# Delta-rule attention and gated experts on one core: column steps of a triangular inverse with the next row by itself, key norms by VectorE from half the number's bits, two spreading copies apart

## The chip, the cores and the metric

The kernel runs on one core of a Trainium2 chip. Its time is the device time in microseconds (us), median of the runs. Engine names are those of the profile: PE (TensorE's matmuls) and PEld (its weight loads), DVE (VectorE), ACT (ScalarE), POOL (GpSimd), SP (the engine that issues most DMAs). Each engine takes its own instructions in the order in which the program gives them, and waits where an instruction needs another engine's result.

## What is computed

Four batches, eight heads, 768 tokens, head size 48. First a delta-rule attention, in which a 48x48 state per head is read and corrected at every token; its key is divided by its own norm:

```python
k_n = k / (np.linalg.norm(k, axis=-1, keepdims=True) + 1e-06)
for t in range(S):
    y[:, :, t] = np.einsum('bhd,bhde->bhe', q[:, :, t], state)
    v_old = np.einsum('bhde,bhd->bhe', state, kt)
    state = state + bt[:, :, :, None] * np.einsum('bhd,bhe->bhde', kt, vt - v_old)
```

The result, as 3072 rows of 384 numbers, goes through a router that picks one of four groups and then one of four experts in that group. Each row is multiplied by its expert's two matrices (384x1024, ReLU, 1024x384) and by the two softmax weights. All of it is in float32.

## The kernel before

**Tiling.** The sequence is cut into NCH = 24 chunks of C = 32 tokens. A chunk holds all four batches (4 x 32 = 128 partitions) and all eight heads. Within a chunk the token-by-token recurrence becomes a lower triangular system of 32x32 per batch and head. Chunks are taken in NGR = 6 groups of RG = 4: the systems of one group, 4 chunks x 8 heads x 4 batches = 128, lie one on each partition, and VectorE inverts them together.

**`gram(u)`** (L209) multiplies chunk u's keys with keys and queries on PE; ACT copies the key part to `gt` (L228), DVE masks the query part into `gq` (L233). Both read one PSUM tile `g_ps`. It shares one buffer (tag "g") with `t_ps` (L385) and `r_ps` (L456), so the next user waits until L233 or L462 has read it.

**`inverse(g)`** (L237) is a generator: a list of steps in which each `yield` hands control back. It transposes `gt` into `m` (L243), takes the squared key norms from the diagonal, then the square root: `max` with a tiny number on DVE (L248), `Sqrt` on ACT (L250), one Newton step on DVE (L252 to L256). It derives the factors `r0` and `norm` (L258 to L270), scales `m` (L272) and prepares `cs` (L277). Then come 30 column steps, j = 1 to 30: a product of column j (rows j+1 and below) with row j (columns 0 to j-1) into `t` (L284), and its addition to the rows below (L288). Every row below j is changed by every step j. Last it multiplies by `cs` (L290), sets the diagonal (L292), transposes into `mt` (L295), and ACT spreads `mt` with two scaled copies into `mtb` (L300), one after the other. Only when `mtb` is there may the next group pass its TURN (L274).

**The period.** `advance(u)` (L315) is chunk u's own work, a chain through PE and ACT: `a_ps` (L321, L327; it reads `vh`, which `scale(u)` makes on DVE at L308) and `f` (ACT L331); `w_ps` from `mtb` (L343) and `w` (ACT L346); the state's update `s_ps` (L353) and `s_bd` (ACT L359, two instructions), which the next chunk's L327 reads; the output `o_ps` (L364) and `x` (ACT L368). Beside it run `logits(u-1)` (L378: `t_ps` on PE, `xt` on ACT L389, `l_ps`, `lg` on ACT L395) and `gram(u+9)`. f(u) below means chunk u's L331; the time from f(u) to f(u+1) is called a period.

**`route(r)`** (L398) is another generator: for a group of four chunks it chooses group and expert with some 25 small DVE instructions. They include `hots` (L448), `rk` (L462), `place` (L464) and `mine` (L484), with an `Exp` on ACT (L459), counting on PE (L456, L457), and, for each chunk, POOL's `at` (L489) and PE's sorting product from `at` and `mine` (L495).

**What sets the order.** Nothing is scheduled by the compiler here: the order of each engine's instructions is the order of the calls. `inverse` and `route` are put into the gaps by `work(n)` (L517). Each call gives every task n x 180 x its rate as credit (rate 0.9 for `inverse`, 0.25 for most `route`); a step is taken while the credit is above zero, and costs 180 plus the number that its `yield` names (L515). A step that yields ACT_STEP, PE_STEP, SOON, NEXT, SORT or TURN waits until the loop calls `allow` with that word. In a period (L579 to L617) the calls are: start of `advance`, `scale(u+1)`, work(16), `w`, allow(SORT), `gram(u+9)`, allow(ACT_STEP), work(9), the mask `gq`, work(8), `s_ps` to `x`, allow(PE_STEP), allow(ACT_STEP), allow(SOON), work(12). `inverse(g)` starts at the end of the period u with u = 4(g-2)+2. Groups 0 and 1 begin ahead of the loop (L552 to L578), where nothing but `gram` stands beside them.

**After the loop** comes the expert stage (L690 to L784): 16 experts in turn, gathering rows by indirect DMA, two matrix products, scattering the results.

Of the kernel before, what the change touches and what calls it, by code (L numbers as in the profile page):

```python
# [8 lines left out]
F32 = mybir.dt.float32  # L9
I32 = mybir.dt.int32  # L10
AX = mybir.AxisListType
ALU = mybir.AluOpType
ACT = mybir.ActivationFunctionType
PSUM = bass.MemoryType.PSUM

C = 32
# [46 lines left out]
def deltanet_then_moe(  # L63
# [13 lines left out]
    nc = tc.nc  # L77
# [76 lines left out]
    with ExitStack() as first:  # L154
# [54 lines left out]
        def gram(u, home=None):  # L209


            g, uu = divmod(u, RG)
            kqt = kqt_[u % NB]
            if uu == 0:
                gts[g] = wk.tile([128, C, RG, H], F32, tag="gt", name=f"gt{g}", bufs=1)
            g_ps = home
            if home is None:
                g_ps = ps.tile([128, 2, 512], F32, tag="g", name=f"g_ps{u}")
            g_out = g_ps.rearrange("p f (j x) -> p (f j) x", j=NP)[:, :, 0:2 * C].rearrange(
                "p h (a t) -> p h a t", a=2)  # L220
            for j in range(NP):
                for b in range(B):
                    for hh in range(2):
                        rows = slice(hh * 64, hh * 64 + D)
                        nc.tensor.matmul(g_out[quads[b], hh * NP + j], lhsT=kqt[rows, 0, j, quads[b]],  # L225
                                         rhs=kqt[rows, :, j, quads[b]], start=True, stop=True,
                                         skip_group_check=True)
            nc.scalar.activation(  # L228
                gts[g][:, :, uu].rearrange("p t h -> p h t"), g_out[:, :, 0, :],
                ACT.Copy)  # L230
            gq = wk.tile([128, H, C], F32, tag="gq", name=f"gq{u}", bufs=LEAD + 1)
            gqs[u] = gq
            return lambda: nc.vector.tensor_tensor(  # L233
                gq, g_out[:, :, 1, :], cut["upper"][:, None, :].to_broadcast([128, H, C]),
                op=ALU.mult)

        def inverse(g):  # L237

            m = wk.tile([128, C, C], F32, tag="m", name=f"m{g}")
            flat = m.rearrange("p i j -> p (i j)")
            nc.vector.transpose(out=flat, in_=gts.pop(g).rearrange("p t u h -> p (t u h)"))  # L243
            yield C * C
            diag = flat[:, ::C + 1]
            nrm, r0, r1 = [sm.tile([128, C], F32, tag=n, name=f"{n}{g}")
                           for n in ("nrm", "r0", "r1")]
            nc.vector.tensor_tensor(r0, diag, cut["tiny"].to_broadcast([128, C]), op=ALU.max)  # L248
            yield ACT_STEP
            nc.scalar.activation(r0, r0, ACT.Sqrt)  # L250
            yield SOON
            nc.vector.reciprocal(r1, r0)  # L252
            yield
            nc.vector.tensor_tensor(r1, r1, diag, op=ALU.mult)
            yield
            nc.vector.tensor_tensor(r0, r0, r1, op=ALU.add)  # L256
            yield
            nc.vector.scalar_tensor_tensor(nrm, in0=r0, scalar=-0.5,  # L258
                                           in1=cut["eps"].to_broadcast([128, C]), op0=ALU.mult,
                                           op1=ALU.subtract)  # L260
            yield
            nc.vector.reciprocal(r1, nrm)
            yield
            nc.vector.tensor_tensor(r1, r1, r1, op=ALU.mult)
            yield
            nc.vector.scalar_tensor_tensor(r0, in0=r1, scalar=-1.0, in1=bt[:, g], op0=ALU.mult,
                                           op1=ALU.mult)
            yield
            norm[g] = sm.tile([128, C], F32, tag="normt", name=f"normt{g}")
            nc.vector.transpose(out=norm[g], in_=nrm)  # L270
            yield
            nc.vector.tensor_tensor(m, m, r0[:, :, None].to_broadcast([128, C, C]), op=ALU.mult)  # L272
            yield C * C
            while g and g - 1 not in mts:  # L274
                yield TURN
            cs = wk.tile([128, C, C], F32, tag="cs", name=f"cs{g}", bufs=1)
            nc.vector.tensor_tensor(cs, cut["below"].rearrange("p (i j) -> p i j", i=C),  # L277
                                    r0[:, None, :].to_broadcast([128, C, C]), op=ALU.mult)
            yield C * C
            for j in range(1, C - 1):  # L280
                n = C - 1 - j
                t = wk.tile([128, C * C // 4], F32, tag="t", name=f"t{g}_{j}")
                tv = t[:, 0:n * j].rearrange("p (i c) -> p i c", i=n)
                nc.vector.tensor_tensor(tv, m[:, j + 1:, j:j + 1].to_broadcast([128, n, j]),  # L284
                                        m[:, j:j + 1, 0:j].to_broadcast([128, n, j]),
                                        op=ALU.mult)
                yield n * j
                nc.vector.tensor_tensor(m[:, j + 1:, 0:j], m[:, j + 1:, 0:j], tv, op=ALU.add)  # L288
                yield n * j
            nc.vector.tensor_tensor(m, m, cs, op=ALU.mult)  # L290
            yield C * C
            nc.vector.tensor_scalar(diag, r0, -1.0, None, op0=ALU.mult)  # L292
            yield
            mt = wk.tile([128, RG * H, C], F32, tag="cs", name=f"mt{g}", bufs=1)
            nc.vector.transpose(out=mt.rearrange("p r i -> p i r"), in_=flat)  # L295
            mtb = wk.tile([128, RG * H, 2, C], F32, tag="mtb", name=f"mtb{g}")
            yield 2 * C * C
            yield ACT_STEP
            for a in range(2):
                nc.scalar.activation(mtb[:, :, a], mt, ACT.Copy,  # L300
                                     scale=cut["parity"][:, a:a + 1])
            mts[g] = mtb
# [204 lines left out]
        def push(task):  # L507
            said = next(task, "end")
            if said == "end":
                behind.remove(task)  # L510
                held.pop(task, None)
                allow(TURN)
            else:
                held[task] = said if isinstance(said, str) else None
                due[task] -= 180 + (said if isinstance(said, int) else 0)  # L515

        def work(n):  # L517

# [10 lines left out]
        def allow(what):  # L529

            for task in list(behind):
                if held.get(task) is what:
                    push(task)
# [4 lines left out]

        with tc.manual_schedule(engines={mybir.EngineType.PE, mybir.EngineType.DVE,
                                         mybir.EngineType.Activation, mybir.EngineType.Pool}):  # L540
            nc.scalar.activation(rooted, cut["tiny"], ACT.Sqrt)
            homes = [None, s_ps[:, 0:2], s_ps[:, 2:4]]
            masks = []
            for u in range(RG):
# [34 lines left out]
            for u in range(NCH + 1):  # L579
                step = advance(u) if u < NCH else iter([None] * 4)  # L580
                turned = logits(u - 1) if u else iter([None] * 2)
                next(step)
                allow(NEXT)
                r = group_of.get(u - 2)
                if r is not None and group_of.get(u - 1) != r and r < NGR - 2:
                    start(route(r), 0.25)
                next(turned)
                if u + 1 < NCH:
                    scale(u + 1)
                work(16)  # L590
                next(step)
                allow(SORT)
                masks = gram(u + LEAD) if u + LEAD < NCH else lambda: None
                allow(ACT_STEP)
                work(9)
                masks()
                work(8)
                next(step)
                next(turned)
                next(step)  # L600
                allow(PE_STEP)
                allow(ACT_STEP)
                r = group_of.get(u - 1)
                if r is not None and group_of.get(u) != r and r >= NGR - 2:
                    start(route(r), 0.6 if r == NGR - 2 else 1)
                allow(SOON)
                if u % RG == RG - 2 and u // RG + 2 < NGR:
                    start(inverse(u // RG + 2), SHARE)
                work(12)
                if u + NB < NCH:  # L610
                    load_kq(u + NB)
                if u + NV < NCH:
                    load_kv(u + NV)
                if u < NCH:
                    nc.sync.dma_start(out=x_dram[u * 128:(u + 1) * 128], in_=xs[u])
                if pieces and u >= RG:
                    pieces.pop(0)()  # L617
# [265 lines left out]
```

## Time and profile before

| what | us |
|---|---|
| median of 3 runs (582.28, 583.00, 584.39) | 583.0 |
| the profiled execution's own time | 588.25 |
| its span, first to last instruction | 586.5 |
| f(0), the first chunk's L331 | 55.3 |
| f(4), f(8), f(12), f(16), f(20) | 97.2, 130.8, 175.5, 212.6, 246.3 |
| f(23), the last chunk's L331 | 270.0 |
| first expert product (L706) | 294.1 |
| DVE busy in the whole span | 251.1 |
| of it L284 and L288, 180 instructions each | 60.3 and 60.0 |

In a timeline row the columns are start in us, duration in us, engine, line, operation, result <- operands with their sizes, and in brackets the idle time before it with what ended it. A duration runs from an instruction's start to its end. Two instructions of one engine may overlap, so the distance from start to start is read beside the duration. The granted clock (PEclk) is the share of full speed at which PE was allowed to run. The mean of the profiled execution was 0.955, but in a stretch it is 1.0 or about a half.

### The profile page before, as it was taken

The page shows a single profiled execution, that of the slowest core. Times are in us where ns is not written, and L with a number is a line of the kernel's source. Part 1 is how long each engine was busy: PE and PEld are TensorE (multiplying, and loading weights), DVE is VectorE, ACT ScalarE, POOL GpSimd, SP SyncE. Part 2 cuts the span into 40 slices and gives each one's busy share as a digit, 9 for nine tenths or more (in the row PEclk, how much of TensorE's full clock was granted, in tenths as well). Part 3 has the DMA queues.
Part 4 walks back from the last instruction along what each step waited for, and adds up shares of the span by engine and source line. Part 5 has one row for each costly group of instructions (what it writes and reads, how often), then busy time and mean ns, then how long its engine had stood idle before and what let it go on. Part 6 is the DMA issues. An engine that isn't in the chain of part 4 may idle for free.

```text
span 586.5 us, 18265 instructions
## 1 busy us (share of the span) xinstructions
PE 503.2 (86%) x8166; PEld 460.1 (78%) x8166; DVE 251.1 (43%) x751; ACT 171.4 (29%) x335; POOL 105.2 (18%) x110
## 2 busy tenths in 40 slices
PE   3213888988999979999599999999999999999993
PEld 2212667767777767778499999999999999999993
DVE  1788997989769879513441011111111111111110
ACT  2102345573564564543011121111111111111110
POOL 0000000002102121121334113414125222221111
PEclk9999998996979989899589999999999999999998
DMA  7990243432421222210126665666756666776400
GB/s 271 403 381 11 83 130 125 160 130 83 143 106 51 90 69 83 82 61 30 36 72 207 181 222 164 215 190 212 249 175 216 213 221 222 242 236 209 169 20 19
DMA packets 44321, 90.64 MB, mean 155 GB/s; under 512 B 9755, under 2 KB 29650, under 8 KB 44240
## 3 DMA queue, kind: packets, MB, share of 16 engines
q1 hardware_dynamic: 34256, 79.71, 40.0%
q0 software_dynamic: 9984, 9.74, 6.2%
q8 instruction: 65, 1.06, 0.8%
q14 instruction: 16, 0.13, 0.1%
HBM read 79.92 MB, written 9.66 MB: 153 GB/s over the span
## 4 chain that ended last, share of the span: by engine, by line
issue 33%; PE 23%; DVE 15%; POOL 12%; DMA 9%; ACT 6%; POOLq 0%; SPq 0%; ACTq 0%
DMA out_dram<-yo,to_i 8%; POOL xg L685 7%; POOL out_dram L736 5%; DVE t L284 4%; DVE m L288 4%; PE a_ps L321 3%; ACT s_bd L359 3%; PE w_ps L343 3%; PE s_ps L353 3%; PE a_ps L327 3%; PE o_ps L336 2%; PE g_ps L225 2%; PE s_ps L495 2%; PE t_ps L385 1%; DMA kqt<-in_kq_dram 1%
## 5 line engine op out<-in xcount | busy, mean ns | idle before, releaser
L706 PE MATMUL h_ps<-xt,w 128*128 128x224 f32 (+14 forms) x768 | 140.4, 337 | 0.6 <-DVE xt L697 0.6
L720 PE MATMUL y_ps<-hid,w 128*128 128x224 f32 (+14 forms) x768 | 138.8, 334 | 0.0
L706 PEld LDWEIGHTS h_ps<-xt,w 128*128 128x128 f32 x768 | 131.3, 192 | 1.6 <-DVE xt L697 0.9
L720 PEld LDWEIGHTS y_ps<-hid,w 128*128 128x128 f32 x768 | 129.3, 190 | 0.3
L697 DVE COPY xt<-t_ps 128x336 f32<-128x336 f32 (+14 forms) x32 | 15.1, 471 | 141.3 <-PE t_ps L695 141.3
L709 ACT ACTIVATE hid<-h_ps 128x448 f32<-128x448 f32 (+14 forms) x64 | 32.3, 505 | 126.9 <-PE h_ps L706 126.9
L735 DVE TENSOR_SCALAR yo<-o_ps,gate 112x384 f32<-112x384 f32 (+14 forms) x32 | 19.6, 616 | 106.3 <-PE o_ps L732 106.3
L284 DVE TENSOR_TENSOR t<-m 128x30 f32<-128x30 f32 (+9 forms) x180 | 60.3, 335 | 4.0
L288 DVE TENSOR_TENSOR m<-m,t 128x30 f32<-128x30 f32 (+9 forms) x180 | 60.0, 334 | 4.5
L685 POOL DMA_INDIRECT xg<-x_dram,from_i x32 | 39.2, 1225 | 115.8 <-PE t_ps L695 100.4
L736 POOL DMA_INDIRECT out_dram<-yo,to_i x32 | 39.2, 1225 | 101.9 <-DVE yo L735 101.0
L321 PE MATMUL a_ps<-vh,con 128*128 128x384 f32 x48 | 26.5, 639 | 33.3 <-DVE vh L308 21.8
L722 ACT ACTIVATE yt<-y_ps 128x224 f32<-128x224 f32 (+14 forms) x48 | 16.2, 338 | 120.2 <-PE y_ps L720 120.2
L359 ACT ACTIVATE s_bd<-s_ps 48x768 f32<-48x768 f32 x46 | 36.9, 803 | 17.6 <-PE s_ps L353 17.0
L321 PEld LDWEIGHTS a_ps<-vh,con 128*128 128x128 f32 x48 | 8.2, 214 | 36.5 <-DVE vh L308 19.9
L489 POOL TENSOR_SCALAR at<-con,place 128x256 f32<-128x256 f32 x20 | 19.9, 1001 | 89.7 <-DVE t L284 36.7
L450 POOL TENSOR_TENSOR acc<-acc,hots 128x16 f32<-128x16 f32 x20 | 5.7, 287 | 147.8 <-DVE hots L448 146.6
L343 PEld LDWEIGHTS w_ps<-f,mtb 64*64 64x64 f32 x768 | 25.6, 139 | 7.1 <-issue 4.9
L343 PE MATMUL w_ps<-f,mtb 64*64 64x48 f32 x768 | 28.9, 224 | 1.7 <-ACT f L331 1.1
L327 PEld LDWEIGHTS a_ps<-s_bd,kqt 128*32 128x32 f32 x736 | 18.1, 125 | 15.5 <-issue 15.5
L353 PE MATMUL s_ps<-w,kv 32*128 32x96 f32 x736 | 28.4, 293 | 0.5 <-issue 0.3
L353 PEld LDWEIGHTS s_ps<-w,kv 32*128 32x128 f32 x736 | 24.4, 198 | 3.1 <-issue 1.0
(115 smaller groups left out, 526.1 us busy)
## 6 DMA issues: line engine op xcount, KB each, us to landing
w<-in_w_dram SPq DMA_DIRECT2D x28, 1536.0 KB, 7.5
kqt<-in_kq_dram SPq DMA_DIRECT2D x24, 512.0 KB, 4.9
kv<-in_kv_dram SPq DMA_DIRECT2D x24, 448.0 KB, 3.4
x_dram<-x SPq DMA_DIRECT2D x24, 192.0 KB, 2.1
w<-in_w_dram SPq DMA_DIRECT2D x6, 512.0 KB, 9.6
w<-in_w_dram SPq DMA_DIRECT2D x4, 576.0 KB, 10.1
w<-in_w_dram SPq DMA_DIRECT2D x2, 384.0 KB, 9.6
con<-in_const_dram SPq DMA_DIRECT2D x1, 512.0 KB, 8.7
```

The lines of the kernel that those rows point to most:

```text
L284: nc.vector.tensor_tensor(tv, m[:, j + 1:, j:j + 1].to_broadcast([128, n, j]), m[:, j:j + 1, 0:j].to_broadcast([128, n, j]), op=ALU.mult)
L288: nc.vector.tensor_tensor(m[:, j + 1:, 0:j], m[:, j + 1:, 0:j], tv, op=ALU.add)
L321: nc.tensor.matmul(a_ps.rearrange("p h d -> p (h d)"), lhsT=ident, rhs=vh.rearrange("p h d -> p (h d)"), start=True, stop=(u == 0), skip_g ...
L327: nc.tensor.matmul(a_ps[quads[b], 2 * j:2 * j + 2, :], lhsT=kqt[:, 0, j, quads[b]], rhs=s_bd[:, b, j], start=False, stop=True, skip_group_ ...
L343: nc.tensor.matmul(w_ps[b, h], lhsT=mt[b, uu * H + (h % 2) * NP + h // 2], rhs=f[b, h], start=True, stop=True, skip_group_check=True)
L353: nc.tensor.matmul(s_at[:, b, j], lhsT=k[quads[b], j], rhs=w[quads[b], 2 * j:2 * j + 2], start=(u == 0 and j == 0), stop=True, skip_group_ ...
L359: nc.scalar.activation(s_bd[rows, :, :, hh, :], s_at[rows, :, :, hh * D:(hh + 1) * D], ACT.Copy)
L685: nc.gpsimd.indirect_dma_start(out=xg[0:P, t, :], out_offset=None, in_=x_dram[:, :], in_offset=bass.IndirectOffsetOnAxis(ap=rows[0:P, t:t ...
L706: nc.tensor.matmul(h_ps[:, k], lhsT=w1[:, j, (f + k) * 128:(f + k + 1) * 128], rhs=xt[:, j], start=(j == 0), stop=(j == DC - 1), skip_grou ...
L709: nc.scalar.activation(hid[:, f:f + 2], h_ps, ACT.Relu)
L720: nc.tensor.matmul(y_ps, lhsT=w2[:, f, j * 128:(j + 1) * 128], rhs=hid[:, f], start=(f == 0), stop=(f == FC - 1))
L736: put = nc.gpsimd.indirect_dma_start(out=out[:, :], out_offset=bass.IndirectOffsetOnAxis(ap=to[0:P, i:i + 1], axis=0), in_=yo[:, :], in_of ...
```

## The change

Line numbers move: after the change, L284 and L288 become L316 and L322, with new lines L294 and L299 in between; L295 becomes L329, L300 L334, L308 L342, L484 L518, L495 L529.

```diff
-            nc.vector.tensor_tensor(r0, diag, cut["tiny"].to_broadcast([128, C]), op=ALU.max)
-            yield ACT_STEP
-            nc.scalar.activation(r0, r0, ACT.Sqrt)
-            yield SOON
+            nc.vector.tensor_scalar(r0.bitcast(I32), diag.bitcast(I32), 0.5, float(0x1fbd1df5),
+                                    op0=ALU.mult, op1=ALU.add)
+            yield
+            nc.vector.reciprocal(r1, r0)
+            yield
+            half = 0.5 * (1 - 3.13e-4)
+            nc.vector.scalar_tensor_tensor(r1, in0=r1, scalar=half, in1=diag, op0=ALU.mult,
+                                           op1=ALU.mult)
+            yield
+            nc.vector.scalar_tensor_tensor(r0, in0=r0, scalar=half, in1=r1, op0=ALU.mult,
+                                           op1=ALU.add)
+            yield
             nc.vector.reciprocal(r1, r0)
...
+            def add_column(j, c):
+                rows = m[:, j + 1:, c]
+                nc.vector.scalar_tensor_tensor(rows, in0=m[:, j + 1:, j], scalar=m[:, j, c:c + 1],
+                                               in1=rows, op0=ALU.mult, op1=ALU.add)
+
+            def add_row(j, i):
+                row = m[:, i, 0:j]
+                nc.vector.scalar_tensor_tensor(row, in0=m[:, j, 0:j], scalar=m[:, i, j:j + 1],
+                                               in1=row, op0=ALU.mult, op1=ALU.add)
+
             for j in range(1, C - 1):
-                n = C - 1 - j
-                t = wk.tile([128, C * C // 4], F32, tag="t", name=f"t{g}_{j}")
-                tv = t[:, 0:n * j].rearrange("p (i c) -> p i c", i=n)
-                nc.vector.tensor_tensor(tv, m[:, j + 1:, j:j + 1].to_broadcast([128, n, j]),
-                                        m[:, j:j + 1, 0:j].to_broadcast([128, n, j]),
-                                        op=ALU.mult)
-                yield n * j
-                nc.vector.tensor_tensor(m[:, j + 1:, 0:j], m[:, j + 1:, 0:j], tv, op=ALU.add)
-                yield n * j
+                n = C - 2 - j
+                if j < 3:
+                    for c in range(j):
+                        add_column(j, c)
+                        yield n + 1
+                elif n < 2:
+                    for i in range(j + 1, C):
+                        add_row(j, i)
+                        yield j
+                else:
+                    t = wk.tile([128, C * C // 4], F32, tag="t", name=f"t{g}_{j}")
+                    tv = t[:, 0:n * j].rearrange("p (i c) -> p i c", i=n)
+                    below = m[:, j + 2:, 0:j]
+                    nc.vector.tensor_tensor(tv, m[:, j + 2:, j:j + 1].to_broadcast([128, n, j]),
+                                            m[:, j:j + 1, 0:j].to_broadcast([128, n, j]),
+                                            op=ALU.mult)
+                    yield n * j
+                    add_row(j, j + 1)
+                    yield j
+                    nc.vector.tensor_tensor(below, below, tv, op=ALU.add)
+                    yield n * j
...
-            yield ACT_STEP
             for a in range(2):
+                yield ACT_STEP
                 nc.scalar.activation(mtb[:, :, a], mt, ACT.Copy,
                                      scale=cut["parity"][:, a:a + 1])
...
-                due[task] -= 180 + (said if isinstance(said, int) else 0)
+                due[task] -= 100 + (said if isinstance(said, int) else 0)
...
-            nc.scalar.activation(rooted, cut["tiny"], ACT.Sqrt)
+            nc.scalar.activation(rooted, cut["tiny"], ACT.Exp)
...
+                allow(ACT_STEP)
                 masks = gram(u + LEAD) if u + LEAD < NCH else lambda: None
-                allow(ACT_STEP)
```

In words, per group of four chunks:

- **The norm.** DVE halves the number's bits and adds a constant, which gives a rough square root, and refines it with one more Newton step (reciprocal, product, sum). ACT's `Sqrt` and the `max` are gone.
- **Column steps.** Steps 1 and 2 are one or two instructions, each of which multiplies a column by one number of each partition and adds it. Steps 29 and 30 do the same by rows. Steps 3 to 28 take three instructions: the product for rows j+2 and below, then row j+1 by itself (product and sum in one instruction), then the addition to rows j+2 and below. That is 84 instructions where there were 60.
- **The two copies into `mtb`** each wait for an allow(ACT_STEP) of their own, and the one in the middle of a period stands ahead of `gram` instead of behind it.
- **The credit** that a step of `inverse` or `route` costs is 100 plus its size instead of 180.
- **The first table** that ACT loads is that of `Exp`.

## The prediction

> **What bounds the kernel now.** First the slices of the span (14.7 us each).
>
> ```profile
> PE   3213888988999979999599999999999999999993
> DVE  1788997989769879513441011111111111111110
> PEclk9999998996979989899589999999999999999998
> ```
>
> DVE is full in the first four slices while PE idles, both are near full up to slice 17, and from slice 20 only PE works. There the expert stage runs PE without a gap (233 of 233 us between 300 and 533), and the change doesn't touch it. Of 586.5 us some 290 are open. PE's clock falls in slices 8, 9, 11 and 14, inside the stage that is open.
>
> Next DVE's timeline, read from start to start.
>
> ```profile
> 22.00 0.42 DVE L233 TENSOR_TENSOR gq<-g_ps,con 128x256 f32<-128x256 f32 x1
> 22.33 0.19 DVE L284 TENSOR_TENSOR t<-m 128x30 f32<-128x30 f32 x1
> 22.55 0.21 DVE L288 TENSOR_TENSOR m<-m,t 128x30 f32<-128x30 f32 x1
> ...
> 106.60 0.40 DVE L284 TENSOR_TENSOR t<-m 128x238 f32<-128x238 f32 x1
> 106.91 0.17 DVE L424 TENSOR_TENSOR gh<-lg,gb 128x16 f32<-128x16 f32 x1
> 107.03 0.41 DVE L288 TENSOR_TENSOR m<-m,t 128x238 f32<-128x238 f32 x1
> ```
>
> A duration is about 157 ns plus 1.04 ns per element. An instruction that needs the one just before starts about 30 ns after that one's end: N elements cost 187 + 1.04N ns (L284 to L288: 0.22). One that doesn't starts while its forerunner still runs: 0.33 after L233, whose 256 elements take 267 ns, so 62 + 1.04N. A stranger between two dependent ones (L424) is free: 106.60 to 107.03 is 0.43, no more than without it.
>
> The prelude, ahead of the first chunk, is DVE alone, but for one wait.
>
> ```profile
> 26.42 0.33 DVE L288 TENSOR_TENSOR m<-m,t 128x168 f32<-128x168 f32 x1
> 30.83 0.42 DVE L233 TENSOR_TENSOR gq<-s_ps,con 128x256 f32<-128x256 f32 x1 [4.08 <-ACT gt L228]
> ...
> 52.53 0.53 DVE L308 TENSOR_TENSOR vh<-kv,normt 128x384 f32<-128x384 f32 x1
> ```
>
> That mask waits for the last early `gram`, which stood 3.48 us in the middle for nothing that the profile shows. Then 21.7 us of DVE to the first `vh`.
>
> In the loop an undisturbed period takes 8.0 us with `gram`, 8.4 with L495 too, 7.7 without `gram`. From f(0) to f(23) the 214.7 us hold some 29 more. Two places carry most of it. ACT in chunk 11:
>
> ```profile
> 165.03 0.49 ACT L346 ACTIVATE w<-w_ps 128x384 f32<-128x384 f32 x1 [0.77 <-PE w_ps L343]
> 166.45 0.62 ACT L228 ACTIVATE gt<-g_ps 128x256 f32<-128x256 f32 x1 [0.92 <-PE g_ps L225]
> 166.86 2.15 ACT L300 ACTIVATE mtb<-mt,con 128x1024 f32<-128x1024 f32 x2
> 169.01 1.28 ACT L250 ACT_TABLE_LOAD   x1
> 170.44 1.62 ACT L359 ACTIVATE s_bd<-s_ps 48x768 f32<-48x768 f32 x2
> ```
>
> Both copies, a table and the root stand ahead of `s_bd`. Elsewhere it follows the end of L228 by 0.55, here by 3.37: 2.8 us late. And PE in chunks 8 and 9:
>
> ```profile
> 135.09 1.06 PE L495 MATMUL s_ps<-mine,at 128*128 128x48 f32 x4 [1.45 <-DVE mine L484]
> 136.07 1.19 PE L225 MATMUL g_ps<-kqt 48*32 48x64 f32 x64
> 137.19 2.04 PE L353 MATMUL s_ps<-w,kv 32*128 32x96 f32 x32
> ...
> 148.60 1.15 PE L353 MATMUL s_ps<-w,kv 32*128 32x96 f32 x32
> ```
>
> A wait of 1.45 us for `mine`, then the same products at half the clock (granted 0.60, 0.50, 0.62 in 134 to 146). From L495 to the next f this took 10.05 us against 6.32 one period later: the low clock cost 3.7. A shorter low stretch (94 to 98) cost 1.3: a_ps 1.65 for 0.91, L327 to L336 1.28 for 0.69.
>
> **Column steps.** A pair costs 374 + 2.08N' ns, N' = j(31-j). Summed over 30 steps (sum of N' 4960) that is 21.5 us per group. In the changed program's order each of the three instructions of a step waits for the one two places before it: the addition for the product, the next product for the row, the row for the last addition. So product to addition costs 187 + 1.04N with the row free between them (62 + 62 + at most 29 is under 187), and addition to next product only 62 + 1.04N: 249 + 2.08N with N = j(30-j). For steps 3 to 28 (sum 4381) that is 6.5 + 9.1 = 15.6 us. The seven others: 1.1. Together 16.7, so **4.9 us less** per group.
>
> The row takes its factor from memory per partition. No row shows that form right behind another. The nearest is L489, also a per-partition factor, 0.18 us after `mine` of 96 elements (62 + 100 ns): no extra. I take none; the upper end is a row that waits for its forerunner and holds its successor, priced below.
>
> [...] Where every one of the 84 pays 187 ns, a group costs 84 x 187 + 9.6 = 25.3 us, 3.8 more than before. The rows above show 62 instead of 187 where nothing depends, and I go by the row.
>
> **Norm.** Four dependent instructions of 32 numbers (three at 0.22, the reciprocal at 0.38) replace L248 and the trip to ACT: 1.04 against 0.49 in group 0, 0.82 in group 1, up to 4.3 with other work between, later. +0.5, +0.2, then a small gain. Halving bits as integers is not in the trace; between 0.19 (other 32s) and 0.31 (an integer shift, L670), I take 0.22. ACT loses five table loads (1.28 each) and six roots.
>
> **Route steps and masks** lose their free places, since the rows occupy them: some 25 at 62 to 130 ns, about 2 us per group. By this spacing in the changed order, four periods with a route cost DVE 31.7 us against 32.9. PE needs 32 to 33.6. DVE just comes clear of PE.
>
> **Copies.** The cheaper credit ends each inverse about half a period earlier. In the new order the first copy stands in chunk 4k+2 between `w` and L228, the second at the end of that period, where they were in 4k+3. The first fits the 0.9 us that ACT idles there, with 0.2 to 0.4 left over; the second (1.09) fits the 1.45 between `x` and the next f, with `Exp` beside it. A late `mt` would hold `gram`'s copy, `s_bd` and PE behind the first one.
>
> **The sum.** *Prelude:* the mask after the product of step 10 is reached at 27.7, waits to 30.83 as before, and then 16.35 us of DVE are left (steps 11 to 28: 4.5 + 6.7; last steps 0.5; masks and rest of step 10: 1.3; L290, L292, L295: 3.3). First `vh` at 47.2 instead of 52.5, f(0) at 50.2. *Chunk 1* waits for its `vh`, behind nine column steps of group 1 where there were seven (a step costs less credit): 11.8 us after the first instead of 11.3. f(1) 63.0, f(2) 71.6. *Chunk 2:* `mt` is ready at 76.3, `w` at 74.7; the first copy waits, s_bd is 1.8 late. f(2) to f(6): 4 x 8.0 + 1.8 = 33.8. *Route pairs:* `mine` can't move, since the mask `gq` ahead of it must wait for chunk 6's own L228 (f(6) + 4.7). Then come 8.25 us: mask 0.33, transpose 1.25, norm 3.65, L272 and L277 2.3, route steps 0.7. So L495 starts at f(6) + 13.0, w_ps being done at + 10.4: PE waits 2.6, and f(8) = f(6) + 13.0 + 6.3 = +19.3. The same in chunks 11 and 15. f(6) to f(10): 19.3 + 16.8 = 36.1; to f(14) 36.4; to f(18) 34.8 (no `gram` from 15); to f(23) 38.5. That gives f(23) = 251.2 at full clock.
>
> [...] I go by the rows: 1.4 for chunk 2 and 2.5 (between 1.3 and 3.7) for each of three waits, 8.9. f(23) = 260.1, 9.9 earlier than 270.0. All behind it moves along: span 576.6, time 578.4 for 588.25. The median of before lies 5.25 under its profiled execution, so 583.0 - 9.9 = **573**.
>
> **Rivals.**
> - *Clock stays up* (the rule, 20%): 573 - 8.9 = 564. For it: DVE and ACT no longer disturb PE elsewhere. [...]
> - *A new wait eats the loop's gain* (20%): each L495 wait and chunk 2 draw the long low stretch, 3.7 each: 573 + 3 x 1.2 + 2.3 = 579. The prelude's 5 stay.
> - *Slower: the flush is paid* (10%): the per-partition factor makes the rows hold their neighbours, so the rule's 25.3 us hold. DVE then needs 32.9 + 3.8 + 0.8 = 37.5 per four periods and bounds the loop, with 1.5 for the mask's wait 39, against 38 on average between f(3) and f(19): +4; prelude +3.4, group 1 +4: 594. It decides from the point at which a step's three instructions cost more than the pair did, 374 + 2.08N'.
> - *It doesn't do what it says* (5%): waits one place apart at run time, or new handshakes cancel the 10 us: 583.
>
> Forecast 45%. A run tells about 0.5% (2.9 us) from no change. Faster: 45 + 20 + 15 of the 579 case = 80%. Same: 5 of that case and 4 of the last = 9%. Slower 11%. The range reaches from 562 (the first rival, less 2 for the low stretch at 278 to 299, which can shift either way) to 580, just past the second; left out are mainly the slower cases.
>
> **What would show it.** From one L322 to the next L316 62 + 1.04N ns, about 0.30 at 225 elements, and L299 hidden. First `vh` near 47. No ACT_TABLE_LOAD past the first. L334 (the copies) in chunks 2, 6, 10 once after `w` and once after `x`, and `s_bd` on time but in chunk 2. `mine` as the releaser of a wait of 2 to 3 us on PE in chunks 7, 11, 15, with low clock behind it. Wrong would make me: steps of 0.5 us more, an L342 that PE waits for in the loop, or a first `vh` later than 50.

## The result, and the profile after

| what | before | after |
|---|---|---|
| median of the runs | 582.8 (4 runs, 582.28 to 584.39) | 582.8 (4 runs, 582.09 to 583.69) |
| the profiled execution's own time, span | 588.25, 586.5 | 582.09, 580.3 |
| f(0), f(3), f(7) | 55.3, 84.9, 121.5 | 51.5, 85.8, 118.6 |
| f(11), f(15), f(23) | 162.7, 201.6, 270.0 | 159.2, 197.8, 264.6 |

The ratio is 0.9996, interval 0.9972 to 1.002: no change, where 573 was forecast, with 562 to 580 as the range. The profiled executions alone differ by 6.2 us. That contradiction is the first thing to explain.

The slices of after, in the order of those shown of before:

```profile
PE   3315779979989899997599999999999999999993
DVE  1889989898898896123531111110111111111110
PEclk9999979989979979998599999999999999999998
```

DVE is as full as before (251.8 us busy for 251.1), but done about one slice earlier: counted from 0, its last high digit is the 6 of slice 15, where before has a 5 in slice 16, and the last group's `mt` starts at 225.09 where it started at 237.58. PE's clock did not get better in the loop: it is low in slices 5, 8, 11 and 14, where before has its low digits in 6, 9, 11, 14 and 16. DVE's timeline shows the new column steps:

```profile
64.22 0.38 DVE L316 TENSOR_TENSOR t<-m 128x224 f32<-128x224 f32 x1
64.53 0.23 DVE L299 SCALAR_TENSOR_TENSOR m<-m 128x14 f32<-128x14 f32 x1
64.67 0.38 DVE L322 TENSOR_TENSOR m<-m,t 128x224 f32<-128x224 f32 x1
64.97 0.38 DVE L316 TENSOR_TENSOR t<-m 128x225 f32<-128x225 f32 x1
```

From L322 to the next L316 it takes 0.30, as forecast. The row takes 0.14 until L322 starts, where 0.08 (62 ns and 14 numbers) was reckoned, so L316 to L322 is 0.45 instead of 0.42, and a step of this size 0.75 instead of 0.715. L322 starts 0.14 behind a row that itself takes 0.23, so the 187 ns are not paid on each instruction.

ACT in chunk 2 and PE in chunk 7:

```profile
76.10 0.49 ACT L380 ACTIVATE w<-w_ps 128x384 f32<-128x384 f32 x1 [0.74 <-PE w_ps L377]
79.30 1.15 ACT L334 ACTIVATE mtb<-mt,con 128x1024 f32<-128x1024 f32 x1 [2.71 <-DVE mt L329]
80.36 0.58 ACT L228 ACTIVATE gt<-g_ps 128x256 f32<-128x256 f32 x1
80.74 1.66 ACT L393 ACTIVATE s_bd<-s_ps 48x768 f32<-48x768 f32 x2
```

```profile
123.96 0.62 PE L529 MATMUL s_ps<-mine,at 128*128 128x48 f32 x4 [2.99 <-DVE mine L518]
...
125.50 2.04 PE L387 MATMUL s_ps<-w,kv 32*128 32x96 f32 x32
127.46 1.47 PE L427 MATMUL l_ps<-wr,xt 128*128 128x20 f32 x6
...
135.43 0.86 PE L225 MATMUL g_ps<-kqt 48*32 48x64 f32 x64
136.22 1.15 PE L387 MATMUL s_ps<-w,kv 32*128 32x96 f32 x32
137.29 0.84 PE L427 MATMUL l_ps<-wr,xt 128*128 128x20 f32 x6
```

In the first, the copy stands behind `w`, waits 2.71 us for `mt`, and L228 and `s_bd` stand behind the copy. In the second, PE waits 2.99 us for `mine`, and the same products as ten microseconds later then take nearly twice as long: L387 2.04 for 1.15, L427 1.47 for 0.84. Two more such waits, 1.66 and 2.48 us, stand in chunks 11 and 15. From L529 to the next f these three took 8.8, 8.5 and 8.1 us. Undisturbed it is 6.32 (chunk 8), and 5.61 without `gram`, which chunk 15 has no more (chunk 16). The low clock (granted 0.58 from 123.9 to 132, 1.00 from 132 to 140) thus cost 2.5, 2.2 and 2.5.

What the change removed is gone: no ACT_TABLE_LOAD after the first, `s_bd` on time in chunks 6, 10 and 14.

### The profile page after: what moved, and what is told of

It is laid out like the page before. It is cut to its first block, busy times and chain, and to the rows that moved or that the text cites. A ratio compares the mean times of both kernels' runs of the same rounds, so it can differ in the third digit from the quotient of the medians.

```text
span 580.3 us, 18417 instructions
## 1 busy us (share of the span) xinstructions
PE 502.1 (87%) x8166; PEld 459.6 (79%) x8166; DVE 251.8 (43%) x913; ACT 164.4 (28%) x324; POOL 105.0 (18%) x110
## 4 chain that ended last, share of the span: by engine, by line
issue 32%; PE 21%; DVE 19%; POOL 12%; DMA 9%; ACT 5%; POOLq 0%; SPq 0%; ACTq 0%; DVEq 0%
DMA out_dram<-yo,to_i 8%; POOL xg L719 7%; POOL out_dram L770 5%; DVE m L322 3%; DVE t L316 3%; PE s_ps L387 3%; PE w_ps L377 3%; PE a_ps L355 3%; ACT s_bd L393 3%; PE a_ps L361 2%; DVE m L299 2%; PE s_ps L529 2%; PE o_ps L370 2%; PE l_ps L427 1%; PE t_ps L419 1%
## 5 line engine op out<-in xcount | busy, mean ns | idle before, releaser
L719 POOL DMA_INDIRECT xg<-x_dram,from_i x32 | 39.3, 1227 | 121.5 <-PE t_ps L729 100.1
L316 DVE TENSOR_TENSOR t<-m 128x81 f32<-128x81 f32 (+13 forms) x156 | 51.3, 329 | 0.2
L322 DVE TENSOR_TENSOR m<-m,t 128x81 f32<-128x81 f32 (+13 forms) x156 | 50.6, 324 | 0.0
L355 PE MATMUL a_ps<-vh,con 128*128 128x384 f32 x48 | 26.2, 633 | 26.0 <-DVE vh L342 15.2
L299 DVE SCALAR_TENSOR_TENSOR m<-m 128x29 f32<-128x29 f32 (+27 forms) x174 | 39.2, 228 | 0.4
L355 PEld LDWEIGHTS a_ps<-vh,con 128*128 128x128 f32 x48 | 8.4, 219 | 28.7 <-DVE vh L342 15.4
L377 PEld LDWEIGHTS w_ps<-f,mtb 64*64 64x64 f32 x768 | 25.3, 138 | 7.0 <-issue 4.9
L387 PE MATMUL s_ps<-w,kv 32*128 32x96 f32 x736 | 28.8, 296 | 0.2
L484 POOL TENSOR_TENSOR acc<-acc,hots 128x16 f32<-128x16 f32 x20 | 5.1, 256 | 129.2 <-DVE hots L482 128.0
```

Of the source, the lines that this page charges most:

```text
L299: nc.vector.scalar_tensor_tensor(row, in0=m[:, j, 0:j], scalar=m[:, i, j:j + 1], in1=row, op0=ALU.mult, op1=ALU.add)
L316: nc.vector.tensor_tensor(tv, m[:, j + 2:, j:j + 1].to_broadcast([128, n, j]), m[:, j:j + 1, 0:j].to_broadcast([128, n, j]), op=ALU.mult)
L322: nc.vector.tensor_tensor(below, below, tv, op=ALU.add)
L355: nc.tensor.matmul(a_ps.rearrange("p h d -> p (h d)"), lhsT=ident, rhs=vh.rearrange("p h d -> p (h d)"), start=True, stop=(u == 0), skip_g ...
L377: nc.tensor.matmul(w_ps[b, h], lhsT=mt[b, uu * H + (h % 2) * NP + h // 2], rhs=f[b, h], start=True, stop=True, skip_group_check=True)
L387: nc.tensor.matmul(s_at[:, b, j], lhsT=k[quads[b], j], rhs=w[quads[b], 2 * j:2 * j + 2], start=(u == 0 and j == 0), stop=True, skip_group_ ...
```

## The experiments

Theory T (T1 in the texts on record, the rivals are R there): the work that the change saves on DVE is real, but PE and ACT get new waits from the order in which steps are placed (`mine` in the middle of a period, a copy that waits for `mt`), each with a stretch of half clock behind it, and the baseline was read from an execution that was slower than usual. Rivals, one for each part: the saving is not there; the low clock comes anyway; the place of a step is all and the change brings nothing; the equality is chance.

The f times of every run's profile, and the medians with the ratio to the kernel before on the same chip:

| run | f(0) | f(3) | f(7) | f(15) | f(23) | median | ratio, interval |
|---|---|---|---|---|---|---|---|
| before2 | 54.3 | 85.5 | 121.3 | 200.7 | 269.1 | (587.35 once) | |
| before3 | 54.0 | 85.2 | 118.3 | 197.1 | 264.0 | (582.26 once) | |
| after2 | 50.1 | 84.5 | 117.5 | 197.5 | 264.3 | 582.0 | 0.9985 (0.9962 to 1.0008) |
| after_fed | 50.0 | 84.4 | 117.9 | 194.4 | 259.1 | 576.8 | 0.9909 (0.9877 to 0.9941) |
| vh_early | 50.0 | 83.3 | 118.3 | 198.0 | 264.9 | 582.6 | 1.0005 (0.9986 to 1.0023) |
| cols_only | 51.0 | 85.7 | 124.3 | 207.6 | 274.6 | 590.5 | 1.0107 (1.0065 to 1.0149) |
| norm_only | 53.9 | 83.0 | 117.9 | 199.7 | 269.8 | 587.0 | 1.006 (1.0033 to 1.0087) |
| copies_only | 54.6 | 86.3 | 118.6 | 197.4 | 266.4 | 583.0 | 0.9973 (0.9943 to 1.0003) |
| norm_copies | 54.5 | 85.2 | 118.1 | 210.3 | 281.3 | 599.1 | 1.0251 (1.0211 to 1.0291) |
| before_sort | 53.7 | 84.7 | 117.9 | 197.4 | 269.1 | 589.6 | 1.0103 (1.0068 to 1.0137) |
| sort_late | 50.6 | 83.7 | 117.5 | 191.4 | 257.0 | 577.1 | 0.9884 (0.9844 to 0.9925) |
| copy_behind_lg | 49.8 | 82.8 | 115.2 | 194.3 | 260.9 | 579.7 | 0.9959 (0.9934 to 0.9983) |
| sort_copy | 49.8 | 81.9 | 115.0 | 186.9 | 253.4 | 569.3 | 0.9773 (0.9734 to 0.9812) |
| sort_copy_early | 50.7 | 84.0 | 122.3 | 191.6 | 257.0 | 576.6 | 0.9899 (0.9874 to 0.9924) |
| sort_copy_columns | 55.1 | 84.0 | 121.6 | 211.7 | 285.8 | 604.9 | 1.038 (1.0344 to 1.0415) |
| sort_copy_root | 49.2 | 81.7 | 121.4 | 207.7 | 282.8 | 602.3 | 1.0351 (1.0318 to 1.0384) |

### Is the baseline what its profile shows?

The kernel before, unchanged, profiled twice more:

> The kernel before, once more, to see which of its executions is typical. Theory (T1): the profiled execution of before (588.2 us) was an unusual one; this one takes 582 to 584, f(23) stands near 265 instead of 270, and the 5 us are missing in the loop, as fewer or shorter stretches at half clock. Rival (R1): recording a profile costs before some 5 us that it does not cost the changed kernel; then this run's profile shows f(23) near 270 again.

> A third profiled execution of the kernel before. T1 (a profiled execution is a draw like the others, and two fell high): 580 to 586. R (the profile itself adds some 4 us to this kernel): 586.5 to 589 again.

The second profiled execution fell high again (587.35, f(23) 269.1), the rival's numbers; the third fell to 582.26 with f(23) = 264.0, the theory's. So an execution of this kernel can differ by 5 us from the next, and without a profile it does too: 579.2 to 586.9 in 29 runs on one chip, 581.9 to 588.4 in 11 on another. Nor does a profile cost time as a rule: in the 15 other runs of this study the profiled execution lay between 2.2 us below and 3.1 above its run's median, 0.1 above on average. Why two of the three of the kernel before fell high stays open.

The three profiles have the same mean clock, 0.955. Of the 6.0 us between the first and the third, 1.3 stand ahead of f(0): the mask's wait ended at 30.83 in the one and at 29.53 in the other. The rest comes in the loop, where the low stretches lie in other places: the first reached f(10) from f(7) in 32.1 us, the third in 30.0, and f(4) from f(0) in 41.9 against 40.4.

The changed kernel, again on a chip with the kernel before:

> The changed kernel once more, beside the kernel before on the same chip. T1 (the change moves half-clock stretches, it does not shorten the time: the kernel before usually has fewer of them than its profiled execution, the changed kernel always has its own): 581 to 584, ratio 0.993 to 1.002, mean granted clock 0.949 to 0.956 in nearly every run, below the 0.960 that the kernel before shows in most of its runs. R (the equality of the medians came from one chip or a few runs): under 580, ratio under 0.992.

This is what T had: 582.0, and f(23) = 264.3 beside 264.0. The granted clock lay at 0.946 to 0.955 in its twelve runs, median 0.950, and at a median of 0.960 in the 29 runs of before. With this pair, `after2` and `before3`, the loss can be placed. After is ahead by 3.9 us at f(0), by 0.7 at f(3), and by 0.9 at f(7). At f(11) it is behind by 0.5 (157.9 and 157.4), and at f(23) by 0.3.

### Where do the 3.9 us of the prelude go?

```diff
             scale(0)
+            scale(1)
...
-                if u + 1 < NCH:
+                if 0 < u < NCH - 1:
                     scale(u + 1)
```

> The changed kernel with vh of chunk 1 made ahead of the loop, right behind vh of chunk 0, instead of behind nine column steps of group 1. T1 (up to f(3) the stage is bound by DVE, whose mt of group 1 the first copy awaits in chunk 2, so a gain ahead of it is eaten there): f(1) 58 to 60 instead of 64 to 65, f(3) 84 to 86 as before, time 579 to 584. R (the wait for vh is where the prelude's 4 us went): f(3) and all behind it 4 or more earlier, 575 to 578.

T had the time (582.6), but f(3) came at 83.3, earlier than its 84 to 86, and the loss was in another place. f(1) came at 59.2, 4.4 earlier than in after2, and then PE stood, with another row in front of it:

```profile
57.45 0.93 PE L355 MATMUL a_ps<-vh,con 128*128 128x384 f32 x2
58.31 0.87 PE L361 MATMUL a_ps<-s_bd,kqt 128*32 128x96 f32 x32
58.99 0.84 PE L370 MATMUL o_ps<-s_bd,kqt 128*32 128x96 f32 x32
64.38 0.90 PE L419 MATMUL t_ps<-con,x 128*128 128x128 f32 x3 [4.54 <-DVE gq L233]
65.21 1.95 PE L377 MATMUL w_ps<-f,mtb 64*64 64x48 f32 x32
```

`t_ps` shares its buffer with `g_ps`, and the mask that reads `g_ps` stands on DVE behind the column steps of group 1. The wait of 3.28 us for `vh` became one of 4.54 for the mask. Up to f(3) DVE has next to no slack (from 47 to 85 us it waits 1.3 us in all in after2), and most of what PE gained at f(1) was given back at the next thing that it needed from DVE. The 1.2 us that were left at f(3) were gone at f(7), after one more wait of 1.58 us for a mask.

### Does half clock follow the waits, and what does it cost?

Six products of constants in front of the first sorting product of chunks 7, 11 and 15:

```diff
                 yield SORT
+                if g == 0 and r < 3:
+                    for _ in range(6):
+                        nc.tensor.matmul(s_ps[:, 1, H * D:512], lhsT=ident, rhs=ones, start=False,
+                                         stop=True, skip_group_check=True)
```

> The changed kernel with six products of constants put on PE ahead of the first sorting product in chunks 7, 11 and 15, where PE waits 2.99, 1.66 and 2.48 us for mine; they write to a part of PSUM that nothing reads and take about 2 us together, so PE has work through most of each wait. Nothing else moves. T1 (idle waits bring the half clock, and it costs about 2.5, 2.1 and 1.8 us behind these three): no half clock behind L529 in these chunks, mean clock up by 0.007 or more, 5 to 6 us less than the changed kernel: 576 to 578. R (the half clock comes by itself, or the waits cost only their own length): no gain, 582 to 585, since the products themselves add up to 0.5 in chunk 11.

T was right: 5.2 us less than after2, by work that nothing needs. In chunk 11, where after had L529 at 163.64, with L427 at 1.47 and L398 at 1.50 behind it:

```profile
161.43 1.60 PE L530 MATMUL s_ps<-con 128*128 128x128 f32 x12
162.87 0.54 PE L533 MATMUL s_ps<-mine,at 128*128 128x48 f32 x4
163.34 0.86 PE L225 MATMUL g_ps<-kqt 48*32 48x64 f32 x64
164.13 1.15 PE L387 MATMUL s_ps<-w,kv 32*128 32x96 f32 x32
165.21 0.84 PE L427 MATMUL l_ps<-wr,xt 128*128 128x20 f32 x6
165.99 0.88 PE L398 MATMUL o_ps<-w,gq 32*32 32x48 f32 x64
```

PE does not stand up to the end of these rows, and L427 takes 0.84 for 1.47, L398 0.88 for 1.50. The period of chunk 11 went from 14.4 (after2) to 10.6 and that of chunk 15 from 12.7 to 10.3. The filling does not bring `mine` earlier: the sorting product starts 4.4 us behind f(11) in both runs, and 4.6 and 4.8 behind f(15). What is saved lies behind it, 3.7 and 2.5 us (of these 6.2, 5.2 are left at f(23)), and that is the price of the half clock. In chunk 15 the products took 1.60 us and 1.09 of the wait was left, without half clock behind it (L398 0.88); in chunk 7 1.26 was left, and the half clock came all the same (L398 1.50, the period 14.2 to 13.8). So the waits of 1.7 to 3.0 us of the changed kernel cost 2.2 to 3.6 us each beyond their own length (after and after2). How short a wait must be to cost nothing more is not settled by these runs.

### The places of the sorting product and of the first copy

`sort_late`, the sorting product behind `x`; `copy_behind_lg`, the first copy behind `l_ps`; `sort_copy`, both:

```diff
                 next(step)
-                allow(SORT)
-                allow(ACT_STEP)
                 masks = gram(u + LEAD) if u + LEAD < NCH else lambda: None
...
                 next(step)
                 next(turned)
+                allow(ACT_STEP)
                 next(step)
+                allow(SORT)
                 allow(PE_STEP)
```

> The changed kernel with the sorting products (L529) moved on PE from behind w_ps to behind o_ps, so that the state's update no longer stands behind the wait for mine. T1: the waits of 2.99, 1.66 and 2.48 us in chunks 7, 11, 15 and the half clock behind them (about 2 us each) go: 582.8 - 7 - 6 = 570, and 0.4 us less in every period with a sort (some 16 of them) could give up to 6 more: 564 to 573. Rival (R2): VectorE bounds the loop in any case, and the wait turns up as one for vh or the mask: 579 to 583.

> The changed kernel with the first allow(ACT_STEP) of a period moved from ahead of gram to behind l_ps, so that both copies stand in one period, the first between lg and x, the second behind x. T1 (chunk 2 loses 4.1 us because its first copy waits 2.7 us for mt ahead of L228 and s_bd): f(2) to f(3) falls from 12.1 to 8.5, the copies make f 0.3 to 0.6 late in chunks 7, 11 and 15: 579 to 581, 2 to 3.5 less than the changed kernel. R (two copies and Exp ahead of f in one period cost as much as the wait): 583 or more.

> Both moves: allow(SORT) behind x, and the first allow(ACT_STEP) behind l_ps. In the run with the sorting product late the first copy still waited for mt ahead of gram in chunks 2 (2.3 us) and 14 (2.6 us, then 5 us late with its half clock). T1: both gone, 1.2 us back for two copies in one period: 568 to 572. R (the copies cost as much behind lg, or the wait for mt turns into a wait of f): 575 to 579.

`sort_late` came between theory and rival: the waits for `mine` went, but in chunk 14 the first copy now waited for `mt` by 2.56 us, as in chunk 2 (2.26). The other two hit T in the time, but `copy_behind_lg` not in the place: f(2) to f(3) took 10.45 us where 8.5 was expected. PE paused there for 1.01 us inside L427, for nothing that the profile shows, and half clock followed (L355 1.65 for 0.91). `sort_copy`, with 10.2 there, has the same pause. `sort_copy` at 569.3 is the fastest version of this study, 12.7 us under after2 on the same chip. Chunk 2 on its ACT, to be read beside the rows of after above:

```profile
74.86 0.63 ACT L228 ACTIVATE gt<-g_ps 128x256 f32<-128x256 f32 x1 [0.30 <-PE g_ps L225]
76.03 1.64 ACT L393 ACTIVATE s_bd<-s_ps 48x768 f32<-48x768 f32 x2 [0.54 <-PE s_ps L387]
77.89 0.19 ACT L429 ACTIVATE lg<-l_ps 128x20 f32<-128x20 f32 x1 [0.23 <-PE l_ps L427]
77.98 1.14 ACT L334 ACTIVATE mtb<-mt,con 128x1024 f32<-128x1024 f32 x1
79.17 0.49 ACT L402 ACTIVATE x<-o_ps 128x384 f32<-128x384 f32 x1
```

Nothing that PE's chain needs stands behind the copy any more but `x`, and the copy no longer waits.

`sort_copy` with `scale(1)` as in `vh_early`, and no allow(ACT_STEP) in chunk 2:

> The kernel with both moves (569.3), vh of chunk 1 made ahead of the loop, and no allow(ACT_STEP) in chunk 2, so that group 1's copies come in chunk 3, when mt is there. T1: f(1) near 58, f(3) near 74, f(4) near 83 instead of 90.2, since nothing of PE's chain waits for DVE until chunk 3; part of it is eaten when DVE, 7 us less ahead, becomes late for chunk 6 or 7: 562 to 568. R (DVE bounds the loop, so that an earlier start only turns into waits for mt): 568 to 571.

Theory and rival both missed: 576.6, worse than without. f(1) came at 59.9, f(2) at 76.2 (the same 4.5 us wait for the mask), and the copies of group 1, a chunk later, made DVE wait 4.4 us for `mtb` at its L287. Neither of these two orders bought the start of the loop.

### The parts of the change

In the kernel before, alone: `cols_only` is the column steps and the credit of 100, `norm_only` the norm and the Exp table, `copies_only` the copies apart and allow(ACT_STEP) ahead of `gram`, `norm_copies` the last two together.

> The kernel before with the column steps and their credit of 100 alone: root on ScalarE, both copies in one step, Sqrt table first. T1: the prelude is 4 us shorter, but copies, table loads and the root still hold the state's update, so most chunks where the copies stand lose 2 to 3.5 us: 580 to 584. Rival (R3): the column steps are worth more than the whole change, and the norm on VectorE takes it back: below 578.

> The kernel before with the norm on VectorE and the two copies apart alone: column steps in pairs, credit 180. T1: prelude 0.5 us longer; the copies no longer hold the state's update in chunks 3, 7, 11, 15 (1.5 to 3.5 us each before), the waits for mine grow by a part of that: 577 to 582. Rival (R3): the longer norm on VectorE costs more than the copies bring: 584 or more.

> The kernel before with the norm on VectorE and the Exp table at the start; copies, columns and credit as before. T1 (of the two parts that made 599 together, the copies are the costly one): s_bd is no longer held by table and root, DVE gets about 4 us more per four chunks of steps of its own order but no wait for the root: 579 to 585. R (the norm's longer chain on DVE makes mt late): 588 or more.

> The kernel before with the two copies at an allow(ACT_STEP) each, the first of a period ahead of gram; norm by Sqrt on ACT, columns and credit as before. T1 (mtb is complete half a period or more later; cs of the next group, which DVE has next in its order, waits for it: 9.6 us of DVE idle in the run with norm and copies): 592 to 600, DVE's waits for mtb over 5 us. R (the copies are harmless, the norm did it): 580 to 587.

T missed all four: `cols_only` was slower than theory and rival had it, `norm_copies` fell to the rival's side, `norm_only` between both, and `copies_only` to the rival. The copies alone are harmless (583.0), the norm alone costs 0.6%, and the two together 2.5%. In `norm_copies` DVE waits at L285 for the second copy:

```profile
DVE gb L428 <- ACT lg L403: 17.3, 2, 12.8
DVE gq L233 <- ACT gt L228: 11.1, 6, 3.1
DVE rk L470 <- PE r_ps L465: 9.9, 1, 9.9
DVE cs L285 <- ACT mtb L308: 9.6, 3, 5.7
```

(Line, what it waits for, us in total, times, longest.) T expected that wait of the copies alone, but `copies_only` does not have it. That the root on ACT there keeps the next group from coming to L285 so early would explain it, but is only argued. In `cols_only`, DVE waits 13.5 us for the root and PE up to 4.2 for a mask that stands on DVE behind a group's last steps and its `mt` (118.1 to 119.9).

The other way round, in the order of `sort_copy`: `sort_copy_columns` has the old column steps and credit, `sort_copy_root` the old root.

> The kernel with both moves (569.3) with the column steps and the credit of the kernel before: all else of the change stays. T1 (in this order DVE has to be quick, and the new column steps are what makes it so: 4.9 us a group): 585 to 597, PE waiting for mt and mine again. R (the order alone does it): 569 to 575.

> The kernel with both moves (569.3) with the square root on ACT again (max, Sqrt, its tables). T1 (five tables and roots of 1.6 us each on ACT, on the path of s_bd where they fall between w and f): 573 to 580. R (ACT has room for them in this order): 568 to 572.

T had the direction, but both cost far more than it said: the columns with their credit are worth 35.6 us there, the norm 33.0 (on another chip than `sort_copy`; the ratios to the kernel before, 1.038 and 1.035 for 0.977, say the same). No run has the columns without the credit, so how much of the 35.6 is quicker steps and how much is the other order of steps stays open. With the root on ACT DVE waits for it 20.7 us (five times, up to 9.0); `sort_copy` has no such wait. Here the root comes behind a copy and a table, and DVE, after 4.50 us of waiting, gets it at 130.4:

```profile
127.72 1.14 ACT L326 ACTIVATE mtb<-mt,con 128x1024 f32<-128x1024 f32 x1
128.88 1.28 ACT L252 ACT_TABLE_LOAD   x1
130.17 0.23 ACT L252 ACTIVATE r<-r 128x32 f32<-128x32 f32 x1
```

And the place alone, allow(SORT) behind `x` in the kernel before:

> The kernel before with the one move that helped the changed one: allow(SORT) behind x instead of behind w. T1 (the cheaper column steps are worth time once PE no longer waits for mine in the middle of a period, and the place alone is worth less): the 2.9 us of waits for mine go with the half clock of one or two of them, but both copies, the table and the root still hold s_bd in three chunks: 578 to 582, ratio 0.990 to 0.998. R (the place is all, the change brings nothing): 575 to 578, as the changed kernel with the same move (577.1).

Neither theory nor rival had it: 1.0% slower. There L495 stands behind `s_bd`, whose PSUM tile it adds to, and `s_bd` is the one that the copies and the root make late:

```profile
165.28 0.88 PE L364 MATMUL o_ps<-w,gq 32*32 32x48 f32 x64
168.83 0.62 PE L495 MATMUL s_ps<-mine,at 128*128 128x48 f32 x4 [2.66 <-ACT s_bd L359]
```

So the better place of the sorting product needs the change, and the change needs the better place.

## Why the prediction was wrong, step by step

It missed by 9.8 us, in two nearly independent parts: 5.25 for the level of the kernel before, and 4.4 between the forecast's own time for the changed kernel, 578.4, and the measured 582.8.

**The baseline.** The step that failed: "The median of before lies 5.25 under its profiled execution, so 583.0 - 9.9". It took the gain from one execution and the level from others. The third profile, at the level of the median, shows that the 5.25 were no fixed cost of profiling. Of the forecast gain of 9.9, 6.0 were such a slow draw (270.0 less 264.0): against the third execution the forecast f(23) of 260.1 would have been a gain of 3.9. Of what the clock cost before the prediction noted 3.7 and 1.3 us in two places and still treated the sum as fixed.

**The changed kernel's own sum,** 4.5 us at f(23) (264.6 for 260.1), and 3.7 in the profiled execution's time. Its mechanisms came; most of its terms were too small:

- *Prelude,* f(0) +1.3. From the end of the mask's wait to the first `vh` it took 17.36 us instead of 16.35, since each row costs 0.14, not 0.08. The rest is a draw: the wait ended at 31.48, not 30.83, in after, and at 30.12 in after2, which so reached the forecast 47.2 and 50.2 almost to the point (47.46 and 50.1), by luck.
- *Chunk 1,* +0.7: 13.5 instead of 12.8.
- *Chunk 2,* f(2) to f(6) +1.3. It was named, with its cause. The copy waited 2.71 us instead of the 1.6 that 76.3 less 74.7 gives.
- *Route pairs:* `mine` as releaser in chunks 7, 11 and 15, forecast 2.6 each, came with 2.99, 1.66 and 2.48. The clock behind them, forecast 2.5 each (the author's estimate between the 1.3 and 3.7 of before's rows), cost 2.5, 2.2 and 2.5. f(6) to f(18) is +0.7 in all, in part by luck: +1.5 up to f(14), then -0.75.
- *Copies and tables:* as forecast.
- *Rivals:* the one that kept the clock up, at 564, fell: no run shows a loss of 0 behind these three waits; in `after` and after2 it was 2.2 to 3.6 us each, and `after_fed`, in which products fill them, took 5.2 us less than after2. The one at 594 fell too: no run shows 187 ns on each of the 84 instructions, and so none its 25.3 us a group. From L322 to L316 it took 0.30, and a step at 224 elements 0.75, where 187 + 1.04N for each of its three instructions would be 1.04. The nearest was "a new wait eats the loop's gain": the waits came, at the size of the forecast and not of the rival's 3.7 (3.6 once, in after2's chunk 11), and against a baseline of 264 that was enough to eat all of it.

Two readings of before's slices were off as well, though no sum rests on them: its clock is low in 6, 9, 11, 14 and 16, not in 8, 9, 11 and 14, and DVE is near full up to 15, not 17.

The mask and the first `vh`, in after and then in after2:

```profile
31.48 0.42 DVE L233 TENSOR_TENSOR gq<-s_ps,con 128x256 f32<-128x256 f32 x1 [3.64 <-ACT gt L228]
48.84 0.53 DVE L342 TENSOR_TENSOR vh<-kv,normt 128x384 f32<-128x384 f32 x1
...
30.12 0.42 DVE L233 TENSOR_TENSOR gq<-s_ps,con 128x256 f32<-128x256 f32 x1 [3.63 <-ACT gt L228]
47.46 0.53 DVE L342 TENSOR_TENSOR vh<-kv,normt 128x384 f32<-128x384 f32 x1
```

So one cause was exchanged for another: before loses much of its time in chunks 7, 11 and 15 to a late `s_bd`, after to a late `mine`. In `before3`, chunk 15, ACT and then PE, which waits for `lg` behind `s_bd` and goes on at half clock:

```profile
199.62 2.18 ACT L300 ACTIVATE mtb<-mt,con 128x1024 f32<-128x1024 f32 x2
201.80 1.28 ACT L250 ACT_TABLE_LOAD   x1
203.23 1.62 ACT L359 ACTIVATE s_bd<-s_ps 48x768 f32<-48x768 f32 x2
...
205.11 1.65 PE L321 MATMUL a_ps<-vh,con 128*128 128x384 f32 x2 [2.02 <-ACT lg L395]
```

The periods of these three chunks are 12.2, 13.1 and 11.2 us in `before3` and 14.2, 14.4 and 12.7 in `after2`. The other periods from f(7) to f(19) give 3.3 us back, so that the stretch takes 114.3 and 115.8.

## What to carry to other kernels

Before a difference of two profiles is put on a median, profile the baseline more than once: here two executions of one program lay 6 us apart, more than the whole effect. Work taken off an engine pays only where the order of the others lets it: here the column steps with their credit and the norm are worth 33 to 36 us each when the sorting product and the copies stand where nothing critical is behind them, and the whole change is worth nothing in the order that came with it. Here the waits of 1.7 to 3.0 us on PE cost their length and 2.2 to 3.6 us of half clock behind it, and useless products that filled them were cheaper, by 5.2 us in all.

## What the runs showed of the hardware

In the kernel before half clock also followed waits of 2.01 us (up to 209.64, then L327 1.51 for 0.87) and 0.80 (up to 243.56, L327 again 1.51), and a pause of 0.70 (up to 168.36, then L364 1.50 for 0.88), while a wait of 0.92 (up to 128.95) had L321 at its 0.91 behind it. In `sort_late` PE paused for 0.99 us in the middle of one line's products, for nothing that the profile shows, and the products behind it ran at about half speed (L355 1.61 for 0.88):

```profile
139.00 0.52 PE L398 MATMUL o_ps<-w,gq 32*32 32x48 f32 x27
140.52 0.62 PE L398 MATMUL o_ps<-w,gq 32*32 32x48 f32 x37 [0.99 <-issue]
141.06 0.95 PE L529 MATMUL s_ps<-mine,at 128*128 128x48 f32 x4
141.81 1.61 PE L355 MATMUL a_ps<-vh,con 128*128 128x384 f32 x2
```

In `sort_copy` the same place paused for 0.65 us, and the products behind it ran at full speed (L355 0.88). The wait of 1.09 us that was left in chunk 15 of `after_fed` was longer and had no half clock behind it (L398 0.88), so the length of one stretch alone does not decide. Why PE pauses there is open. An instruction with a factor per partition (L299 in the changed kernel) took 0.13 to 0.16 us from its start to the next one's where an ordinary one of its size would take 0.07 to 0.09 by the prediction's 62 + 1.04N. Halving a float's bits as an integer (L250 there) took 0.19, no more than other instructions of 32 numbers.
